# A layer with linear attention and a gated MLP on one core: query features token-major and normalised, turned by DMA; KV sums and numerators in blocks of three heads; a new order of the units

## The chip, the cores and the metric

The kernel runs on one core of a Trainium2 chip. A core has a matrix engine (TensorE, PE in the profile, with its weight loads as PEld), a vector engine (DVE), a scalar engine (ACT), GpSimd (POOL), a synchronisation engine that mainly issues transfers (SP), and 16 DMA engines. The engines run their own instruction streams in order and wait for each other on semaphores. Matrices are multiplied from SBUF into PSUM (eight banks of 512 fp32 columns). The metric is device microseconds of one execution, as a median of several runs. A profiled execution tells where the time goes.

## What is computed

One sequence of 2048 tokens, width 640, 32 heads of 20, all in bf16 at the borders. The layer norm has no learned scale.

```python
def _A_ref(x, wqkv, w_phi, wo):
    H = 32; Dh = D // H
    q, k, v = ...                      # x @ wqkv, split into heads
    pq = jnp.einsum("bhsd,hdf->bhsf", q, w_phi)
    pk = jnp.einsum("bhsd,hdf->bhsf", k, w_phi)
    phi_q = jnp.concatenate([_softmax(pq, axis=-1), _softmax(-pq, axis=-1)], axis=-1)
    phi_k = jnp.concatenate([_softmax(pk, axis=-1), _softmax(-pk, axis=-1)], axis=-1)
    kv = jnp.einsum("bhsf,bhsd->bhfd", phi_k, v)
    z  = jnp.einsum("bhsf->bhf", phi_k)
    num = jnp.einsum("bhqf,bhfd->bhqd", phi_q, kv)
    den = jnp.einsum("bhqf,bhf->bhq", phi_q, z)[..., None] + 1e-6
    return (num / den) ... @ wo
...
h = x + _A_ref(_layernorm(x), ...)
g, u = _layernorm(h) @ w_gate, _layernorm(h) @ w_up     # 640 -> 1536
return h + (g * u) @ w_down                             # 1536 -> 640
```

So each head has 40 features per token: a softmax over 20 numbers and a softmax over their negatives. The KV sum runs over all tokens, so no numerator can be made before the last key tile has been added.

## The kernel before

**Tiles.** 16 token tiles of 128 tokens. Weights of q and k are first multiplied with `w_phi` ("folds", `F1_*` for k and `F0_*` for q, L389), so that features come from one projection. For the folds, K weights are transposed on TensorE (`WT`, L370) and Q weights by DMA (`wqt`, L302).

**Key and value side, per token tile t.** `L1*` and `xn` normalise the tile; `xt` transposes it, for the first four tiles on TensorE (L451), for the others by a DMA on SP's queue (L460). `V` and `K` (L473) are token-major projections: ten matmuls of 320 columns into two PSUM banks, split into five parts for tiles 0 and 1. ACT makes exp(+) and exp(-) of the K projection (`Kx`, L494) into `ek`; DVE sums each group of 20 (`Ks`, L497); ACT makes the reciprocals by Ln and Exp (`Kr`, `Ke`); POOL multiplies (`Kn`, L504). `KV` (L513) adds the tile to the KV sum: 128 feature columns of one sign are the weights, the values of the heads that these 128 columns touch are the moving side (21 columns a head, the 21st being ones, for z). 128 columns touch 7 or 8 heads of 20, and both signs lie apart, so a tile takes 12 matmuls with 1512 columns in all, into three banks. Products of a head's features with another head's values are masked off with `GL` at the end (`KVe`, L520).

**Query side.** `Q` (L534) is feature-major: 20 units, one for each 512 tokens and 128 features, of five matmuls of 512 columns. ACT writes exp(+) and exp(-) straight into `eqT` (`Qx`, L543), which stays unnormalised and needs no transpose. `N` (L567) makes the numerators of a tile, for each sign apart: six matmuls a sign, 22 columns a head (values, z, and a column of ones that gives the softmax sum). DVE then joins the signs, six instructions a tile: `sr` (L580), `rho` (L582), `A` (L585), `B` (L588), `dd` (L592), `rd` (L596); `o` (L599) multiplies with the reciprocal, on POOL or DVE.

**After that, per tile.** `oT` (L604) transposes `o` by DMA, `O` (L610) multiplies with `wo`, `h` (L614) adds x, `L2*` and `hc` make the second layer norm, `hT` (L637) transposes it by DMA into `xnT`, in place of the tile's first normalised copy.

**MLP.** Five blocks of tokens `FB` (256, 512, 512, 512, 256). `U` units (L652) are five matmuls each, gate and up; `g` (ACT, L657) copies the gate, `u` (DVE, L660) multiplies; `D` (L671) is the down projection of a tile, 24 matmuls of 320 columns; `y` (L683) adds h, `w` (L685) stores. `wd` loads `w_down` into the space of the q, k and v weights, and so waits for the last projection.

**Order.** `build_graph` makes named operations, with their engine. The list `TUNED` gives each a number; `schedule` walks through the graph in the order of these numbers and assigns buffers, `emit` turns dependencies into semaphore waits. What is built is one fixed list of instructions for each engine: each engine, SP's queue too, runs its list in order, so one that waits holds all behind it.

Of the kernel before, what the change touches and what calls it, by code (L numbers as in the profile page):

```python
# [12 lines left out]
P = 128  # L13
# [16 lines left out]
for _s in range(2):  # L30
    for _c in range(NC):
        OFF[_s, _c] = _o
        _o += NH[_c]
NSLOT = _o
BSLOT = NSLOT // 3

QB = [(512 * b, 512) for b in range(4)]
# [18 lines left out]
L1a12:33.687 L1s13:28.597 L1a13:31.337 L1s14:33.797 L1a14:35.117 L1s15:26.247 L1a15:28.487 L1l0:7.437 L1e0:7.867 L1l1:4.317 L1e1:4.747 L1l2:11.156
L1e2:11.586 L1n2:11.896 L1n3:12.096 L1l4:15.157 L1e4:16.001 L1n4:16.711 L1n5:16.511 L1n6:16.311 L1n7:16.911 L1l8:26.088 L1e8:26.667 L1n8:28.855
L1n9:31.414 L1n10:31.814 L1n11:31.614 L1l12:35.45 L1e12:35.88 L1n12:39.691 L1n13:36.932 L1n14:36.732 L1n15:39.491 xn0:8.226 xt0:9.088 xte0:9.853
xn1:5.057 xt1:5.737 xte1:6.905:1 xn2:12.348 xt2:13.039 xte2:13.911 xn3:12.574:1 xt3:13.59 xte3:15.748:1 xn4:17.487 xt4:20.107 xn5:17.348:1 xt5:18.887
xn6:16.987 xt6:17.667 xn7:17.987 xt7:21.327 xn8:29.417 xt8:30.097 xn9:31.764:1 xt9:32.687 xn10:33.25:1 xt10:35.127 xn11:34.617 xt11:36.347 xn12:40.341  # L60
xt12:41.227 xn13:37.588:1 xt13:40.007 xn14:37.082 xt14:38.787 xn15:39.841 xt15:44.887 V0_0:10.806 V0_1:11.078 V0_2:11.681 V0_3:11.953 V0_4:12.496
Ve0:13.287 K0_0:14.141 K0_1:14.412 K0_2:14.684 K0_3:14.956 K0_4:15.227 Kx0_0:16.101 Kx0_1:18.684 Ks0:19.907 Kr0:21.568 Ke0:22.431 Kn0:24.137 KV0:29.083
V1_0:9.44 V1_1:9.712 V1_2:12.224 V1_3:12.768 V1_4:13.869 Ve1:14.534 K1_0:7.713 K1_1:8.817 K1_2:10.263 K1_3:10.534 K1_4:13.318 Kx1_0:15.377 Kx1_1:16.724
Ks1:18.487 Kr1:20.554 Ke1:21.418 Kn1:21.778 KV1:29.759 V2:19.574 Ve2:24.691 K2:15.499 Kx2_0:18.061 Kx2_1:19.308 Ks2:21.327 Kr2:23.204 Ke2:25.314
Kn2:26.496 KV2:33.151 V3:16.857 Ve3:19.931 K3:18.216 Kx3_0:20.794 Kx3_1:21.808 Ks3:24.827 Kr3:26.427 Ke3:27.39 Kn3:29.055 KV3:33.827 V4:30.435
Ve4:32.477 K4:26.366 Kx4_0:27.994 Kx4_1:28.907 Ks4:29.917 Kr4:31.517 Ke4:33.1 Kn4:34.373 KV4:37.22 V5:23.649 Ve5:25.464 K5:27.724 Kx5_0:30.029
Kx5_1:30.862 Ks5:32.267 Kr5:34.587 Ke5:35.67 Kn5:37.132 KV5:40.613 V6:22.291 Ve6:24.068 K6:20.933 Kx6_0:22.581 Kx6_1:23.444 Ks6:27.067 Kr6:28.667
Ke6:29.53 Kn6:32.014 KV6:45.364 V7:25.008 Ve7:26.767 K7:31.793 Kx7_0:33.963 Kx7_1:34.827 Ks7:35.66 Kr7:38.302 Ke7:38.752 Kn7:39.891 KV7:47.398
V8:35.862 Ve8:37.582:1 K8:34.503 Kx8_0:36.132 Kx8_1:36.965 Ks8:38.333 Kr8:40.148 Ke8:41.011 Kn8:42.25 KV8:48.389 V9:39.254 Ve9:40.883:1 K9:37.896
Kx9_0:39.524 Kx9_1:40.388 Ks9:41.634 Kr9:43.54 Ke9:43.99 Kn9:44.609 KV9:49.065 V10:41.289 Ve10:42.917 K10:42.647 Kx10_0:44.275 Kx10_1:45.109  # L70
Ks10:45.942 Kr10:47.542 Ke10:48.405 Kn10:48.765 KV10:52.789 V11:54.824 Ve11:56.452:1 K11:46.04 Kx11_0:47.782 Kx11_1:48.615 Ks11:49.449 Kr11:51.085
Ke11:51.535 Kn11:53.483 KV11:60.257 V12:53.465 Ve12:55.207 K12:50.072 Kx12_0:51.7 Kx12_1:52.534 Ks12:53.367 Kr12:54.967 Ke12:55.83 Kn12:56.19
KV12:60.933 V13:58.899 Ve13:60.527:1 K13:51.43 Kx13_0:53.157 Kx13_1:53.99 Ks13:54.824 Kr13:56.424 Ke13:56.874 Kn13:58.549 KV13:62.239 V14:56.182
Ve14:57.81 K14:44.005 Kx14_0:45.732 Kx14_1:46.565 Ks14:47.399 Kr14:49.862 Ke14:50.312 Kn14:51.124 KV14:62.915 V15:63.906 Ve15:65.534 K15:57.54
Kx15_0:59.169 Kx15_1:60.002 Ks15:61.279 Kr15:62.879 Ke15:63.329 Kn15:63.689 KV15:68.502 KVe0:70.058 KVe1:70.668 KVe2:69.448 F0_0:48.074 Fe0_0:49.239
F0_1:61.609 Fe0_1:62.194 F0_2:63.591 Fe0_2:64.176 F0_3:49.741 Fe0_3:50.462 F0_4:61.924 Fe0_4:62.699:1 Q0_0:70.257 Qx0_0_0:71.606 Qx0_0_1:72.123
Q0_1:67.423 Qx0_1_0:69.288 Qx0_1_1:68.772 Q0_2:69.178 Qx0_2_0:70.527 Qx0_2_1:71.044 Q0_3:66.343 Qx0_3_0:67.693 Qx0_3_1:68.209 Q0_4:65.264 Qx0_4_0:67.13
Qx0_4_1:66.613 Q1_0:74.529 Qx1_0_0:75.879 Qx1_0_1:76.395 Q1_1:76.689 Qx1_1_0:78.039 Qx1_1_1:78.555 Q1_2:73.45 Qx1_2_0:75.316 Qx1_2_1:74.799 Q1_3:91.923
Qx1_3_0:93.974 Qx1_3_1:93.457 Q1_4:78.459 Qx1_4_0:80.324 Qx1_4_1:79.808 Q2_0:88.34 Qx2_0_0:90.357 Qx2_0_1:90.874 Q2_1:71.336 Qx2_1_0:72.685
Qx2_1_1:73.202 Q2_2:90.844 Qx2_2_0:92.94 Qx2_2_1:92.424 Q2_3:89.764 Qx2_3_0:91.39 Qx2_3_1:91.907 Q2_4:82.041 Qx2_4_0:83.39 Qx2_4_1:83.907 Q3_0:79.538  # L80
Qx3_0_0:80.887 Qx3_0_1:81.404 Q3_1:80.617 Qx3_1_0:82.483 Qx3_1_1:81.966 Q3_2:87.261 Qx3_2_0:89.84 Qx3_2_1:88.61 Q3_3:75.61 Qx3_3_0:76.959
Qx3_3_1:77.476 Q3_4:83.12 Qx3_4_0:84.469 Qx3_4_1:84.986 wd0:94.712 wd1:94.232 wd2:93.272 wd3:93.752 N0_1:73.105 N0_0:72.415 sr0:73.72 rho0:74.21
A0:74.58 B0:75.61 dd0:76.64 rd0:77.03 o0:77.51:1 oT0:78.422 O0:84.199 h0:86.035 L2s0:87.087 L2a0:88.659 L2v0:88.949 L2r0:89.659 hc0:89.127 hT0:90.05
N1_1:77.769 N1_0:72.76 sr1:78.384 rho1:78.874 A1:79.244 B1:80.274 dd1:81.304 rd1:81.694 o1:82.174:1 oT1:83.085 O1:85.903 h1:87.907 L2s1:88.839
L2a1:89.839 L2v1:90.129 L2r1:90.844 hc1:90.344:1 hT1:91.27 N2_1:89.419 N2_0:85.558 sr2:90.034 rho2:90.974 A2:91.344 B2:92.374 dd2:93.404 rd2:93.794
o2:94.274 oT2:95.695 O2:103.382 h2:105.142 L2s2:106.555 L2a2:107.727 L2v2:108.017 L2r2:111.472 hc2:108.017 hT2:108.94 N3_1:81.696 N3_0:78.114
sr3:82.905 rho3:83.395 A3:83.765 B3:84.795 dd3:85.825 rd3:86.787 o3:87.267 oT3:88.688 O3:93.002 h3:94.63 L2s3:95.692 L2a3:96.702 L2v3:96.992
L2r3:97.732 hc3:97.261 hT3:98.184 N4_1:94.36 N4_0:94.705 sr4:95.382 rho4:96.512 A4:96.882 B4:98.214 dd4:99.415 rd4:99.805 o4:100.457:1 oT4:101.369
O4:112.592 h4:114.437 L2s4:115.369 L2a4:116.369 L2v4:116.659 L2r4:117.159 hc4:116.659:1 hT4:117.622 N5_1:100.308 N5_0:98.325 sr5:101.189 rho5:101.679
A5:102.049 B5:103.25 dd5:104.452 rd5:104.842 o5:105.322 oT5:106.743 O5:110.889 h5:112.555 L2s5:113.617 L2a5:115.189 L2v5:115.479 L2r5:116.189  # L90
hc5:115.479 hT5:116.402 N6_1:105.286 N6_0:106.177 sr6:106.245 rho6:107.837 A6:108.207 B6:109.409 dd6:110.61 rd6:111.172 o6:111.652 oT6:113.073
O6:120.47 h6:122.099 L2s6:123.04 L2a6:124.71 L2v6:125 L2r6:125.74 hc6:125.87:1 hT6:126.55 N7_1:145.093 N7_0:143.669 sr7:145.981 rho7:146.471 A7:146.841
# [132 lines left out]
def build_graph():  # L225
# [329 lines left out]
    for t in range(NT):  # L555
# [18 lines left out]
        def nv(b, lo, hi):  # L574
            return pp(b, 0, 352).rearrange("p b (h e) -> p b h e", e=22)[:, :, :, lo:hi]
# [457 lines left out]
```

## Time and profile before

| | us |
|---|---|
| median of 3 runs (281.85 to 282.33) | 282.11 |
| span of the profiled execution | 281.1 |
| TensorE busy in it | 274.9 |
| DVE busy | 176.8 |
| ACT busy | 109.6 |
| POOL busy | 61.3 |
| DMA queue 1, share of 16 engines | 28.9% |

| group | instructions | busy, us | mean of one, ns |
|---|---|---|---|
| `KV` L513, TensorE | 192 | 12.7 | 218 |
| `N` L567, TensorE | 192 | 15.7 | 221 |
| `Q` L534, TensorE | 96 (of 100) | 21.9 | 379 |
| `Ks` L497, DVE | 16 | 23.3 | 1475 |
| `Kn` L504, POOL | 16 | 37.4 | 2358 |
| `Qx` L543, ACT | 40 | 21.4 | 598 |
| `A`, `B` L585 and L588, DVE | 16 each | 13.7 each | 854 |
| `xt`, `hT` L460 and L637, SP | 28 | - | - |

The mean of one matmul is longer than the distance between two starts, since matmuls overlap; the distance is read from the chain of waits or from the starts. A transpose on SP is an issue of some 1.2 us, and the data move after it; the DMA issues of the page give the time to landing.

### The profile page before, as it was taken

The page shows a single profiled execution, that of the slowest core. Times are in us where ns is not written, and L with a number is a line of the kernel's source. Part 1 is how long each engine was busy: PE and PEld are TensorE (multiplying, and loading weights), DVE is VectorE, ACT ScalarE, POOL GpSimd, SP SyncE. Part 2 cuts the span into 40 slices and gives each one's busy share as a digit, 9 for nine tenths or more (in the row PEclk, how much of TensorE's full clock was granted, in tenths as well). Part 3 has the DMA queues.
Part 4 walks back from the last instruction along what each step waited for, and adds up shares of the span by engine and source line. Part 5 has one row for each costly group of instructions (what it writes and reads, how often), then busy time and mean ns, then how long its engine had stood idle before and what let it go on. Part 6 is the DMA issues. An engine that isn't in the chain of part 4 may idle for free.

```text
span 281.1 us, 5047 instructions
## 1 busy us (share of the span) xinstructions
PE 274.9 (98%) x2058; PEld 182.7 (65%) x2075; DVE 176.8 (63%) x357; ACT 109.6 (39%) x217; POOL 61.3 (22%) x78
## 2 busy tenths in 40 slices
PE   7899999999999999999999999999999999999996
PEld 3677777876556688765555675545675554587874
DVE  5899986542588798855888974338725452341532
ACT  3799876846785742112311301303200203330200
POOL 6017998873002102202012000010110200000000
PEclk9999999999999999999999999999999999999999
DMA  7923276990011692232111342010141230000001
GB/s 211 369 56 74 53 131 113 313 372 8 0 26 31 153 261 48 41 79 49 25 23 26 70 106 60 0 23 2 25 97 47 40 32 23 0 2 23 26 34 60
DMA packets 43479, 21.98 MB, mean 78 GB/s; under 512 B 34624, under 2 KB 42176, under 8 KB 43456
## 3 DMA queue, kind: packets, MB, share of 16 engines
q1 hardware_dynamic: 42080, 20.02, 28.9%
q10 hardware_dynamic: 1376, 1.64, 1.9%
q8 instruction: 16, 0.26, 0.4%
q14 instruction: 7, 0.06, 0.1%
HBM read 11.00 MB, written 2.62 MB: 48 GB/s over the span
## 4 chain that ended last, share of the span: by engine, by line
PE 95%; DMA 2%; DVE 1%; issue 0%; ACTq 0%; ACT 0%; POOL 0%; DVEq 0%
PE ps L652 36%; PE ps L671 19%; PE ps L473 16%; PE ps L610 8%; PE ps L534 8%; PE ps L567 4%; PE ps L513 4%; DMA scratch<-in_A_wqkv_dram 2%; PE ps L389 1%; PE ps L370 0%; PE ps L451 0%; DVE x_all L614 0%; DVE ev L660 0%; DVE st L620 0%; ACTq L274 0%
## 5 line engine op out<-in xcount | busy, mean ns | idle before, releaser
L652 PE MATMUL ps<-xnT,Wgu 128*128 128x512 bf16 (+1 forms) x587 | 106.4, 335 | 0.7
L652 PEld LDWEIGHTS ps<-xnT,Wgu 128*128 128x128 bf16 x600 | 58.1, 98 | 41.7 <-DVE ev L660 0.6
L657 ACT ACTIVATE scratch<-ps 128x512 bf16<-128x512 f32 (+1 forms) x60 | 30.7, 512 | 117.4 <-PE ps L652 98.5
L660 DVE TENSOR_TENSOR ev<-ps,scratch 128x512 bf16<-128x512 f32 (+1 forms) x60 | 33.6, 579 | 34.5 <-ACT scratch L657 18.7
L671 PE MATMUL ps<-Wp,ev 128*128 128x320 bf16 (+2 forms) x396 | 53.5, 295 | 0.0
L671 PEld LDWEIGHTS ps<-Wp,ev 128*128 128x128 bf16 x396 | 38.0, 98 | 14.1
L473 PE MATMUL ps<-Wp,xnT 128*128 128x320 bf16 x320 | 45.9, 299 | 0.0
L504 POOL TENSOR_TENSOR ev<-ev,SR 128x1280 bf16<-128x1280 bf16 x16 | 37.4, 2358 | 9.5 <-ACT SR L502 9.5
L473 PEld LDWEIGHTS ps<-Wp,xnT 128*128 128x128 bf16 x320 | 30.7, 98 | 11.2
L599 POOL TENSOR_TENSOR scratch<-scratch,sm 128x640 bf16<-128x640 f32 x10 | 12.7, 1273 | 94.9 <-DVE sm L596 91.7
L683 DVE SCALAR_TENSOR_TENSOR Wp<-ps,rs,x_all 128x640 bf16<-128x640 f32 (+3 forms) x18 | 14.5, 808 | 30.0 <-PE ps L671 30.0
L497 DVE TENSOR_REDUCE SR<-ev 128x64 f32<-128x1280 bf16 x16 | 23.3, 1475 | 6.2 <-ACT ev L494 6.1
L610 PE MATMUL ps<-Wo,scratch 128*128 128x320 bf16 x160 | 24.0, 299 | 0.0
L543 ACT ACTIVATE eqT<-ps 128x512 bf16<-128x512 f32 x40 | 21.4, 598 | 6.2 <-PE ps L534 6.2
L494 ACT ACTIVATE ev<-ps 128x640 bf16<-128x640 f32 x32 | 21.6, 713 | 4.2 <-PE ps L473 3.6
L534 PE MATMUL ps<-xnT,Wp 128*128 128x512 bf16 x96 | 21.9, 379 | 0.2
L610 PEld LDWEIGHTS ps<-Wo,scratch 128*128 128x128 bf16 x160 | 15.6, 98 | 7.0 <-issue 0.2
L614 DVE TENSOR_TENSOR x_all<-ps,x_all 128x640 bf16<-128x640 f32 x16 | 12.9, 813 | 7.8 <-PE ps L610 7.8
L534 PEld LDWEIGHTS ps<-xnT,Wp 128*128 128x128 bf16 x100 | 9.6, 98 | 10.3
L567 PE MATMUL ps<-KVm,eqT 128*128 128x154 bf16 (+1 forms) x192 | 15.7, 221 | 0.0
L567 PEld LDWEIGHTS ps<-KVm,eqT 128*128 128x128 bf16 x192 | 13.0, 98 | 4.0
L624 POOL TENSOR_SCALAR ln<-mv 128x1 f32<-128x1 f32 x16 | 3.3, 210 | 49.4 <-DVE mv L623 47.3
(59 smaller groups left out, 204.4 us busy)
## 6 DMA issues: line engine op xcount, KB each, us to landing
out_dram<-Wp SPq DMA_DIRECT2D x15, 160.0 KB, 1.8
x_all<-in_A_x_dram SPq DMA_DIRECT2D x6, 320.0 KB, 10.0
Wgu<-in_B_w_up_dram SPq DMA_DIRECT2D x5, 384.0 KB, 7.7
Wgu<-in_B_w_gate_dram SPq DMA_DIRECT2D x5, 384.0 KB, 6.1
Wp<-in_B_w_down_dram SPq DMA_DIRECT2D x4, 480.0 KB, 5.2
scratch<-in_A_wqkv_dram ACTq DMA_DIRECT2D x2, 320.0 KB, 5.5
Wo<-in_A_wo_dram SPq DMA_DIRECT2D x1, 480.0 KB, 9.0
xnT<-xn SPq DMA_TRANSPOSE x28, 2.7
```

The source lines that it names most:

```text
L473: ins = e.matmul(pb(b, hb)[:, 0:320], lhsT=T["xnT"][:, NC - 1 - c, P * t:P * (t + 1)], rhs=T["Wp"][:, kind, c, 320 * hb:320 * (hb + 1)], s ...
L494: G.op("act", "Kx%d_%d" % (t, s), lambda e, s=s, b=b, ek=ek: e.activation(out=T["ek"][:, ek.slots[0], s, :].rearrange("p (b n) -> p b n", ...
L497: G.op("dve", "Ks%d" % t, lambda e, ek=ek, sr=sr: e.tensor_reduce(out=T["SR"][:, sr.slots[0], 0, :], in_=T["ek"][:, ek.slots[0], :, :].rea ...
L504: G.op("pool", "Kn%d" % t, lambda e, ek=ek, sr=sr: e.tensor_tensor(out=T["ek"][:, ek.slots[0], :, :].rearrange("p s (h f) -> p (s h) f", f ...
L534: ins = e.matmul(pb(b)[:, 0:n], lhsT=T["Wp"][:, 0, i, P * c:P * (c + 1)], rhs=T["xnT"][:, NC - 1 - i, o0:o0 + n], start=(i == 0), stop=(i ...
L543: G.op("act", "Qx%d_%d_%d" % (q, c, s), lambda e, s=s, c=c, o0=o0, n=n, b=b: e.activation(out=T["eqT"][:, s, c, o0:o0 + n], in_=pb(b)[:, 0 ...
L567: ins = e.matmul(pb(b, y)[:, 22 * h0:22 * (h0 + j1 - j0)], lhsT=T["eqT"][:, s, c, P * t:P * (t + 1)], rhs=T["KVm"][:, OFF[s, c] + j0:OFF[s ...
L610: ins = e.matmul(pb(b, hb)[:, 0:320], lhsT=T["oT"][:, oT.slots[0], c, :], rhs=T["Wo"][:, c, 320 * hb:320 * (hb + 1)], start=(c == 0), stop ...
L652: ins = e.matmul(pb(b)[:, 0:n], lhsT=T["Wgu"][:, gu, c, P * ft:P * (ft + 1)], rhs=T["xnT"][:, NC - 1 - c, o0:o0 + n], start=(c == 0), stop ...
L657: G.op("act", "g%d_%d" % (bi, ft), lambda e, pg=pg, gt=gt, n=n: e.activation(out=T["gt"][:, gt.slots[0], 0:n], in_=pb(pg)[:, 0:n], func=AF ...
L660: o_ = G.op("dve", "u%d_%d" % (bi, ft), lambda e, pu=pu, gt=gt, hh=hh, ft=ft, n=n: e.tensor_tensor(out=T["hh"][:, hh.slots[0], ft, 0:n], i ...
L671: ins = e.matmul(pb(b, hb)[:, 0:w], lhsT=T["hh"][:, hh.slots[0], ft, P * tt:P * (tt + 1)], rhs=T["Wd"][:, ft, c0 + w * hb:c0 + w * (hb + 1 ...
```

## The change

**Query features.** `Q` becomes a token-major projection like K and V, 16 units of ten matmuls of 320 columns. `feat` (new, used for K and Q) makes exp, sums and reciprocals, now with a head's two signs side by side, 40 columns a head. `Qn` multiplies into a buffer `ph` of 11 blocks of 128 columns (three heads are 120 columns, the rest is zeros), on POOL for twelve tiles and on DVE for tiles 0, 1, 2 and 11. `qT` turns all 11 blocks with one DMA transpose on SP's queue.

**KV and numerators.** Weights are 128 columns that hold three heads with both signs; the moving side is these three heads, 63 columns (42 for the last two heads). Eleven matmuls a tile for `KV`, twelve for `N` (block 5 lies across two banks and is split). Two KV banks in place of three. `N` comes once, normalised, so `sr`, `rho`, `A`, `B` go, and `dd`, `rd`, `o` read PSUM; `o` is always on DVE.

**Placement and order.** `eqT`, `A`, `B` go, `ph` (4 buffers), `phT` (5) and a mask come; `ek` has 7 buffers in place of 6, and `SR` 4 in place of 3. The weights of q come last in `Wp`, so that `wd0` to `wd2` wait for the K and V projections alone, `wd3` for Q too. A new list `PLAN` gives every operation a number, its engine and its buffers; `arrange` sorts by the number in place of `schedule`.

```diff
-QB = [(512 * b, 512) for b in range(4)]
+NB = 11
+BW = [120 * g for g in range(10)] + [1152]
+BH = [3] * 10 + [2]
+POS = {1: 0, 2: 1, 0: 2}
...
+    def feat(nm, t, b, kk):
...
+            G.op("act", "%sx%d_%d" % (nm, t, s), lambda e, s=s, b=b, ek=ek: e.activation(
+                out=T["ek"][:, ek.slots[0], :].rearrange("p (b h s f) -> p b h s f", b=2, s=2, f=DH)[:, :, :, s, :],
+                in_=pp(b, 0, 320).rearrange("p b (h f) -> p b h f", f=DH), func=AF.Exp,
+                scale=1.0 - 2.0 * s), act_c(640), LA, [b], [ek], kk)
+        G.op("dve", "%ss%d" % (nm, t), lambda e, ek=ek, sr=sr: e.tensor_reduce(
...
         def kv(e, t=t, ek=ek, va=va):
-            for k in range(3):
-                for n, (s, c, j0, j1, sl) in enumerate(ent[k]):
...
+            for g in range(NB):
+                n = 21 * BH[g]
+                ins = e.matmul(pb(KVB[g // 8])[:, 63 * (g % 8):63 * (g % 8) + n], lhsT=T["ek"][:, ek.slots[0], BW[g]:BW[g] + P],
+                               rhs=T["va"][:, va.slots[0], 63 * g:63 * g + n],
+                               start=(t == 0 and g % 8 == 0), stop=(t == NT - 1), skip_group_check=True)
...
+    for t in range(NT):
+        kk = 165 + 8 * t
+        b = proj(0, t, "Q%d" % t, kk)
+        ek, sr = feat("Q", t, b, kk)
+        ph = Buf("ph%d" % t, "ph")
+        def qn(e, eng, ek=ek, sr=sr, ph=ph):
...
+            e.tensor_tensor(
+                out=o_[:, 0:10 * P].rearrange("p (g n) -> p g n", n=P)[:, :, 0:120].rearrange("p g (h f) -> p g h f", f=DH),
+                in0=i_[:, 0:1200].rearrange("p (g h f) -> p g h f", h=6, f=DH),
+                in1=r_[:, 0:60].rearrange("p (g h) -> p g h", h=6).unsqueeze(3).to_broadcast([P, 10, 6, DH]), op=ALU.mult)
+            return e.tensor_tensor(
...
+        G.op("sp", "qT%d" % t, lambda e, ph=ph, phT=phT: e.dma_start_transpose(
+            out=T["phT"][:, phT.slots[0], :, :], in_=T["ph"][:, ph.slots[0], :]), 2.6, 0.0, [ph], [phT], kk, dma=-2.2)
     for k in range(4):
         dma("sp", "wd%d" % k, lambda k=k: T["Wd"][:, 3 * k:3 * k + 3, :],
...
-            after=lastproj)
+            after=kvprojs if k < 3 else projs)
...
+            for g in range(NB):
+                for h0, h1 in [(3 * g, 3 * g + BH[g])] if g != 5 else [(15, 16), (16, 18)]:
+                    y = h0 // 16
+                    ins = e.matmul(pb(b, y)[:, 21 * (h0 - 16 * y):21 * (h1 - 16 * y)], lhsT=T["phT"][:, phT.slots[0], g, :],
+                                   rhs=T["KVm"][:, h0:h1, :].rearrange("p h e -> p (h e)"),
...
-        G.op("dve", "sr%d" % t, ...
-        G.op("dve", "rho%d" % t, ...
-        G.op("dve", "A%d" % t, ...
-        G.op("dve", "B%d" % t, ...
...
+        G.op("dve", "o%d" % t, lambda e, sm=sm, b=b, o=o: e.tensor_tensor(
+            out=T["o"][:, o.slots[0], :].rearrange("p (b h d) -> p b h d", b=2, d=DH), in0=nv(b, 0, 20),
...
-        order, _ = schedule(G)
+        order = arrange(G)
```

The parts of the new lists that the prediction speaks of, in the order in which the engines run them:

```
SP, start:       x0 x1 wk4 x2 w5 wk2 wk0 wv0 x4 wv2 x6 x14 wv4 x8 x12 x10   (before: two queues, SP and ACT)
POOL, start:     all three Phi products on POOL (before: two on DVE), with the mask among the selects
SP, then:        ... xt15 xt12 wqt4 wu3 wo2 wu0 wg2 wu4 wu1 wg0 wg1 wu2 wo0 wg3 xt13 wg4 xt14 qT2 qT5 qT0 qT1
SP, from V13:    wd1 wd0 wd2 qT4 qT8 oT0 oT1 qT3 qT7 oT4 oT5 oT2 hT0 hT1 qT15 qT6 oT3 qT12 wd3 oT8 hT4 oT7 qT14
                 hT2 hT5 hT3 qT13 qT10 qT9 w1 hT8 qT11 oT15 hT7 oT6 oT10 w0 oT14 oT13 hT6 ...
PE, V9 to K14:   V9 F0_0 KV4 V10 F0_2 F0_4 KV5 KV6 F0_1 F0_3 K11 K15 Q2 Q5 KV7 KV8 Q0, Q1 (in parts) KV9 K12 KV10 K14
PE, from V13:    V13 Q3 KV13 KV14 KV15 Q15 N0 N1 Q9 Q11 N2 N4 Q10 Q13 O0 N5 Q12 N8 O1 N3 Q14 O4 O5 O2 N7
                 24 units U0, with O3 among them, then O8 N6 O7 N15 D1 U1 U1 D0 N14 U1 U1 N10 U1 U1 N11 ...
```

The first unit of U0 needs `hT0` and `hT1`; the first of U1 needs `hT2` to `hT5`. After the last N and O, TensorE has only U and D units left.

## The prediction, made before the changed kernel was run

> **What bounds the kernel now.** I read the page's busy times first, then the slices, then the chain of waits.
>
> ```profile
> PE 274.9 (98%) x2058; PEld 182.7 (65%) x2075; DVE 176.8 (63%) x357; ACT 109.6 (39%) x217; POOL 61.3 (22%) x78
> ...
> PE   7899999999999999999999999999999999999996
> ...
> PEclk9999999999999999999999999999999999999999
> ...
> PE 95%; DMA 2%; DVE 1%; issue 0%; ACTq 0%; ACT 0%; POOL 0%; DVEq 0%
> ```
>
> TensorE is busy from the second slice to the last, at full clock, and it is 95% of the chain. From 15.3 us to the last matmul at 278.3 no start lies later than its predecessor's columns explain; seventeen gaps of 0.22 us are one missing record each. So the end is the start-up, plus the sum of the matmul work, plus whatever idle time a change puts in. The price of the work stands in the chain of waits in order of time:
>
> ```profile
> 30.73 1.36 PE ps L513 x24
> 32.09 2.72 PE ps L473 x20
> ...
> 142.81 0.71 PE ps L567 x12
> 143.52 2.16 PE ps L652 x10
> ...
> 150.71 1.36 PE ps L610 x10
> ```
>
> Columns are: start, us, what, count. Two KV tiles of 12 matmuls (L513) take 1.36, so 0.68 a tile; a projection of ten 320-column matmuls (L473, L610) takes 1.36, 136 ns each; the numerators of a tile (L567) take 0.71; a 512-column matmul (L652, likewise the Q unit L534) takes 216 ns.
>
> **The change, part by part. TensorE.** KV per tile goes from 12 matmuls with 1512 columns to 11 with 672 (ten of 63, one of 42); the numerators from 12 with 1584 columns to 12 with 672. No row has 63 columns. In single starts of the trace a 42-column matmul of L513 holds PE for 29 ns (median of 32), the 80-column ones of L389 for 35 ns, each with a weight load of its own. So 63 lies between 29 and 35; 63 columns at the 42-to-80 slope would be 32, but 80 columns cost 33.3 at 2.4 columns a ns plus 2, and 63 by that is 28. I take 30. KV: 0.68 - 11 x 0.030 = 0.35 less a tile, 5.6 us over 16. Numerators: 0.71 - 0.36 = 0.35, 5.6 us. Q was 100 matmuls of 216 ns = 21.6, and is 160 of 136 = 21.8: 0.2 more. **Net -11.0** (-11.4 at 29 ns, -9.3 at 35).
>
> One rule speaks against this. The Trainium skill, "TensorE: Matmul & The Clock Gate", Back-to-back issue gap, gives some 81 ns per matmul for a stream of weight-load and 128-column matmul pairs; the 128-column transposes L370 and L451 here start 56 ns apart, so the row decides. By the page an estimate for KV would be 11 x 81 = 0.89 us a tile, above the 0.68 of now, and the change would lose on TensorE.
>
> **Vector, scalar and GpSimd work.** DVE loses the two 672-wide passes (L585, L588, 13.7 us each), `sr` and `rho` (5.7 + 2.9) and six `o`; it gains 16 reductions `Qs` (L497's row, 1475 ns: 23.6), 16 `o` from PSUM (L614's row, 813 ns: 13.0) and four `Qn` (about 1.5). ACT trades 40 Exp of 598 ns for 32 of 713 and gets 32 small ones of 0.26; the evictions of V (L238, 711 ns), which write runs of 20 elements already, show that the interleaved output costs no more. POOL trades ten `o` (1273) for twelve `Qn` (by L504's 2358 ns for 1280 elements: about 2.5). `Kn` and `Qn` together are 16 x 2.36 + 12 x 2.5 = 68 us of POOL, from the first Exp pair at some 20 us to `Qn13` at some 110. None of this is on the path while TensorE has other units ready, and I cost it at nothing; what it costs if the cover fails is rival 2, DVE being the fullest of the three between 70 and 125 us.
>
> **SP's queue.** This is where the cover is thin. Each `qT` turns 11 blocks of 128x128, against five in every transpose there is now.
>
> ```profile
> xnT<-xn SPq DMA_TRANSPOSE x28, 2.7
> ...
> 36.29 2.60 SPq L460 DMA_TRANSPOSE xnT<-xn  x2
> 38.93 1.27 SPq L302 DMA_TRANSPOSE scratch<-in_A_wqkv_dram  x1
> 40.24 4.54 SPq L460 DMA_TRANSPOSE xnT<-xn  x3
> ```
>
> The first line is from the DMA issues, the others from the timeline of SP. A five-block transpose holds SP for 1.20 us alone and 1.27 in a dense row, where starts lie 1.31 apart; its packets run from 1.17 to 2.13 us after the issue (0.96 us of transfer) and it lands at 2.7. Eleven blocks aren't shown. If the issue costs per instruction, one holds SP for 1.3; if per block, 11/5 x 1.20 = 2.64 and 0.04 between; if per block as in the slowest instruction there is (the one at 41.57 us took 1.90), 4.2. I take 2.68, since the transfer starts only when the issue is over, as if the issue wrote the descriptors one after another. It lands 2.1 (transfer) + 0.45 later.
>
> In the new order SP works through, after the last K/V projection V13 has freed `Wd`'s space, up to `qT11`: 12 `qT`, 15 five-block transposes, four `wd` and one output. That is 12 x 2.68 + 15 x 1.31 + 2.3 + 2.5 for the last landing = 56.6 us. TensorE's units from V13 to N11, the numerators that wait for `qT11`, are 16 Q and O (21.8), 3 KV (1.0), 12 N (4.3), 24 U0 (0.545 each: 13.1), 2 D (L671, 3.26: 6.5) and 6 U1 (1.08: 6.5): 53.2. **SP is 3.4 us longer than the work that hides it: +3.4 of idle TensorE.** Behind a `qT` that waits stand the `oT` and `hT` that feed O and U, so these come late by the same. At 1.3 per `qT` it is hidden (0); at 2.85 (dense rows) it is 5.4; at 4.2 it is 21.7. The same sum up to `hT1`, before the first U0, gives 21.5 of work against 4 x 2.68 + 7 x 1.31 + 1.5 + 1.4 = 22.8: there the first 1.3 of it show.
>
> "Advanced Engine Details and Errata" of the Trainium skill, X-Bar Transpose (TRN2), says that transposing DMAs are as fast as plain ones, 350 to 400 GB/s. Here 160 KB took 0.96 us, 171 GB/s. By the page an estimate for the 352 KB of a `qT` is 0.95 us in place of 2.1, and the idle time would be 2.3.
>
> **Loads behind which work now waits.** `xt13` and `xt14` are issued behind the Wo, gate and up loads. Those 4.7 MB now go from the first issue at 48.78 to landed data at 63.2, 14.4 us; two transposes add 2 x 0.96 + 0.45: 16.8. Where the loads begin in the new order TensorE is at V9; from there to K14, which needs `xt14`, are nine projections (12.2), five Q folds (1.6) and seven KV (2.3): 16.1. So +0.7 (0 to 1.6).
>
> **Start-up.** All input loads go through SP alone, K weights ahead of V's. In the present trace TensorE waits for K weights until 8.41 (chain: L370) and the last V weights land at 12.8, behind x tiles that aren't needed yet; then it is dense from 15.3. The bytes ahead of the last V weights fall to 3.3 MB, at some 350 GB/s from 2 us on: 11.5 to 12. All three `Phi` products (658 ns on POOL) now stand on POOL behind its memsets and selects, some 5.9 us by their rows in all after 0.8, so at 6.7; the K folds need them at about 7.3, K weights landed, turned and copied. I take -0.5 (-1.5 to +1.0: one queue in place of two, or POOL, may come late).
>
> **Sum.** 281.1 (span) - 11.0 + 3.4 + 0.7 - 0.5 = 273.7. The median of the runs is 1.0 above the span, so **274.7 us**.
>
> **The rivals.** (1) *The transposes are hidden after all* (issue under 2.4 us): the idle 3.4 goes. Time: 271.3. For it: SP is free for long stretches in the present trace; against it: a dense queue with 12 of the new kind. 0.25.
> (2) *DVE becomes the bound in that stretch.* From `Qs6` to `Qn11`, which feeds `qT11`, the new order has 10 reductions (1.40 start to start), 9 `o` and 8 `h` (0.74), 8 pairs of statistics (0.75), 12 `u` (0.335) and small ones: 45.9 us back to back, and 5.2 for `qT11` makes 51.1, under 53.2. At the use DVE reaches in its busiest stretch now (33.29 of 40.00 us between 17 and 57) it takes 55.3 + 5.2 = 60.5: idle 7.3 instead of 3.4, time 278.6. 0.09.
> (3) *Narrow matmuls don't go under the 56 ns of 128 columns.* KV 0.62, N 0.67: TensorE saves 1.4 in all, and its longer units hide SP's 3.4 and the loads' 0.7. Time: 281.1 - 1.4 - 0.5 + 1.0 = 280.2. Against it: the rows of 42 and 80. 0.05.
> (4) *The other side: the 11-block transposes hold SP at the rate of its slowest one*, 4.2 us. Place: the queue from V13 to `qT11`; idle 21.7 instead of 3.4; time 293. It decides from 3.4 + 7.4 = 10.8 us of idle, that is 0.6 us more per `qT` than I take: 3.3. For it: instructions of 1.3 to 1.9 in dense rows; against: one in 49. 0.11.
>
> **How the numbers follow.** The forecast holds 0.48, with 272.5 to 277.5 as its own range; 0.02 is left for no change. A difference under 0.2% (0.6 us) can't be told from none here. Faster: 0.48 + 0.25 + 0.09 + 0.05 = 0.87; slower 0.11. The range takes in (1) less some start-up gain and goes to (3): 270.4 to 280.3.
>
> **What would show it.** L513's and L567's successors at some 0.33 and 0.36 us a tile in the chain; the `qT` lines on SP at 2.6 to 2.7 us; SP without a pause between V13 and `qT11`; holes in TensorE of together 3 to 5 us before the first U0, before U1 and at N11, released by a transpose, and none after about 130 us. No holes, or `qT` at 2.4 or less, means (1). Holes released by DVE mean (2). A gap of 50 ns between 63-column matmuls means (3). `qT` above 3.3 us makes the forecast wrong in sign.

## The result, and the profile after

The changed kernel takes **284.1 us** (median of 7 runs, 283.21 to 285.96); the kernel before took 282.11 in the same session (7 runs, 281.85 to 283.05). The ratio is 1.007, 95% interval 1.0042 to 1.0098: slower by 0.7%, where 2.6% faster was forecast. Here and below a ratio leaves out runs that lie more than 1.5% above the same kernel's fastest, while medians and ranges are of all runs. The profiled execution has a span of 283.5 us. The parts of its page that were read before:

```profile
PE 268.4 (95%) x2119; PEld 179.0 (63%) x2119; DVE 181.1 (64%) x324; ACT 113.3 (40%) x241; POOL 82.6 (29%) x99
...
PE   6999997998939989999999999999999999999996
...
PEclk9999997999988999999999999999999999999999
...
PE 72%; DMA 11%; DVE 8%; issue 3%; ACT 2%; POOL 2%; SPq 1%; DVEq 0%
```

The TensorE line, without a break before, now has breaks in slices 7, 10, 12 and 15, all between 42 and 107 us; the clock line dips in slices 7, 12 and 13; and the chain that ended last is only 72% TensorE. From slice 16 on the kernel is as dense as it was. So the saving and the loss lie in different places, and the saving can be read by itself, in the chain of waits of the changed kernel (start, us, what, count):

```profile
56.71 0.68 PE ps L525 x22
...
106.16 0.35 PE ps L578 x12
```

Two KV tiles of 11 matmuls (L525) take 0.68, 0.34 a tile where it was 0.68 a tile; the numerators (L578) take 0.35 in place of 0.71. The matmul work has become 11 us shorter, as the sum had it. What it met instead stands in TensorE's timeline between 30 and 150 us, in the brackets: idle time before the line, and what ended it.

```profile
33.51 4.25 PE L481 MATMUL ps<-Wp,xnT 128*128 128x320 bf16 x30 [0.48 <-DMA xnT<-xn]
45.53 0.74 PE L408 MATMUL ps<-Phi,scratch 128*128 128x140 bf16 x6 [1.99 <-DMA scratch<-in_A_wqkv_dram]
69.12 4.25 PE L481 MATMUL ps<-Wp,xnT 128*128 128x320 bf16 x30 [1.20 <-ACT ev L250]
83.73 1.86 PE L525 MATMUL ps<-ev,ek 128*128 128x63 bf16 x33 [4.59 <-DVE ev L250]
91.44 0.52 PE L578 MATMUL ps<-KVm,scratch 128*128 128x63 bf16 x12 [0.17 <-DMA scratch<-ph]
103.27 2.89 PE L604 MATMUL ps<-Wo,scratch 128*128 128x320 bf16 x20 [0.72 <-DMA scratch<-o]
```

The largest wait, 4.59 us, is ended by the copy of a V projection on VectorE (L250), and the next, 1.99, by a transpose of Wq out of DRAM. Three small ones are ended by transposes out of SBUF, of which the forecast's sum had counted the last two, a `qT` and an `oT`. At the two large holes TensorE went to half clock: the granted clock is 0.50 from 45.59 to 49.00 us and from 83.13 to 86.55, 3.41 us each time. In these stretches 320-column matmuls started 266 ns apart in place of 136, and 63-column ones 53 in place of 32; the same matmuls took 1.6 and 1.2 us longer than at full clock.

Measured from the distances of matmul starts, each less its own columns at 2.4 a ns and 2.5 ns (single missing records left out), TensorE's idle time per stretch is, in us (what half clock adds counts as idle here):

| kernel | 5 to 16 | 30 to 60 | 60 to 90 | 90 to 150 | last matmul ends |
|---|---|---|---|---|---|
| before | 1.7 | 0.2 | 0.2 | 0.3 | 278.5 |
| changed | 2.4 | 4.7 | 7.6 | 2.3 | 281.2 |

Why VectorE copied V13 so late is seen on VectorE and GpSimd together. L497 is the group sum of the features, L549 and L553 are the two multiplies of a `Qn` (1200 and 80 columns), L517 is `Kn`. From the timeline of the changed kernel:

```profile
61.60 2.40 DVE L553 TENSOR_TENSOR ph<-ek,SR 128x80 bf16<-128x80 bf16 x1
...
69.49 2.01 DVE L549 TENSOR_TENSOR ph<-ek,SR 128x1200 bf16<-128x1200 bf16 x1
...
71.95 4.67 POOL L517 TENSOR_TENSOR ek<-ek,SR 128x1280 bf16<-128x1280 bf16 x2 [1.70 <-ACT SR L502]
...
74.37 3.52 DVE L549 TENSOR_TENSOR ph<-ek,SR 128x1200 bf16<-128x1200 bf16 x1
...
76.58 3.39 POOL L549 TENSOR_TENSOR ph<-ek,SR 128x1200 bf16<-128x1200 bf16 x1
77.81 2.25 DVE L553 TENSOR_TENSOR ph<-ek,SR 128x80 bf16<-128x80 bf16 x1
...
82.77 0.81 DVE L250 CAST ev<-ps 128x640 bf16<-128x640 f32 x1
```

An 80-column multiply of 0.23 us takes 2.40 and 2.25; the 1200-column one, 1.41 alone (at 130 us, when GpSimd rests), takes 2.01 and 3.52. GpSimd's own multiply beside them takes 3.39 in place of 2.22. The times interlock: GpSimd's two `Kn` end at 76.62; VectorE's multiply, issued at 74.37, ends 1.27 us later at 77.89; GpSimd's `Qn`, issued at 76.58, ends 2.08 us after that; and VectorE's 80 columns end 0.09 us after it. The excess on VectorE is 2.2 us for `Qn2`, 0.6 for `Qn0` and 4.1 for `Qn1`: 6.9 us, just ahead of the copy that TensorE waits for.

The theory: **a VectorE multiply with two inputs in SBUF and a GpSimd multiply exclude each other for whole instructions.** The Trainium skill states this, on the page "SBUF — State Buffer", Who interferes with whom: a VectorE instruction with two SBUF inputs contends with a GpSimd instruction that reads SBUF, the later one is held up until the other has ended, and a `tensor_reduce` never contends. The trace agrees: no L497 was longer than 1.49. The rivals: VectorE merely has too much work there; or SP's queue of transposes sets the pace, as the forecast had it.

### The profile page after: what moved, and what is told of

Same layout as the page of the kernel before. It is cut to its first block, busy times and chain, and to the rows that moved or that the text cites. A ratio compares the mean times of both kernels' runs of the same rounds, so it can differ in the third digit from the quotient of the medians.

```text
span 283.5 us, 5219 instructions
## 1 busy us (share of the span) xinstructions
PE 268.4 (95%) x2119; PEld 179.0 (63%) x2119; DVE 181.1 (64%) x324; ACT 113.3 (40%) x241; POOL 82.6 (29%) x99
## 4 chain that ended last, share of the span: by engine, by line
PE 72%; DMA 11%; DVE 8%; issue 3%; ACT 2%; POOL 2%; SPq 1%; DVEq 0%
PE ps L646 35%; PE ps L665 18%; PE ps L481 8%; PE ps L604 6%; DMA scratch<-ph 4%; DVE SR L497 3%; DMA scratch<-o 3%; DMA scratch<-in_A_wqkv_dram 3%; POOL ek L517 2%; DVE ph L549 2%; DMA xnT<-xn 1%; ACT ek L493 1%; PE ps L408 1%; PE ps L578 1%; SPq L284 1%
## 5 line engine op out<-in xcount | busy, mean ns | idle before, releaser
L651 ACT ACTIVATE gt<-ps 128x512 bf16<-128x512 f32 (+1 forms) x60 | 30.6, 512 | 104.2 <-PE ps L646 65.3
L481 PE MATMUL ps<-Wp,xnT 128*128 128x320 bf16 x480 | 70.4, 303 | 1.7 <-ACT ev L250 1.2
L654 DVE TENSOR_TENSOR ev<-ps,gt 128x512 bf16<-128x512 f32 (+1 forms) x60 | 33.3, 578 | 42.8 <-PE ps L646 28.6
L481 PEld LDWEIGHTS ps<-Wp,xnT 128*128 128x128 bf16 x480 | 46.2, 99 | 19.7 <-ACT ev L250 1.5
L497 DVE TENSOR_REDUCE SR<-ek 128x64 f32<-128x1280 bf16 x32 | 46.7, 1474 | 2.2 <-ACT ek L493 2.2
L493 ACT ACTIVATE ek<-ps 128x640 bf16<-128x640 f32 x64 | 43.3, 701 | 11.5 <-PE ps L481 7.1
L517 POOL TENSOR_TENSOR ek<-ek,SR 128x1280 bf16<-128x1280 bf16 x16 | 38.7, 2434 | 15.4 <-ACT SR L502 15.4
L549 POOL TENSOR_TENSOR ph<-ek,SR 128x1200 bf16<-128x1200 bf16 x12 | 27.8, 2319 | 14.1 <-ACT SR L502 10.6
L594 DVE TENSOR_TENSOR o<-ps,sm 128x640 bf16<-128x640 f32 x16 | 12.8, 808 | 3.2 <-DMA scratch<-o 3.1
L525 PE MATMUL ps<-ev,ek 128*128 128x63 bf16 (+1 forms) x176 | 8.1, 204 | 4.6 <-DVE ev L250 4.6
L525 PEld LDWEIGHTS ps<-ev,ek 128*128 128x128 bf16 x176 | 7.8, 106 | 5.5 <-issue 4.9
L250 ACT ACTIVATE ev<-ps 128x640 bf16<-128x640 f32 x13 | 9.2, 707 | 2.2 <-PE ps L481 2.2
```

Of the source, the lines that this page charges most:

```text
L481: ins = e.matmul(pb(b, hb)[:, 0:320], lhsT=T["xnT"][:, NC - 1 - c, P * t:P * (t + 1)], rhs=T["Wp"][:, POS[kind], c, 320 * hb:320 * (hb + 1 ...
L493: G.op("act", "%sx%d_%d" % (nm, t, s), lambda e, s=s, b=b, ek=ek: e.activation(out=T["ek"][:, ek.slots[0], :].rearrange("p (b h s f) -> p ...
L497: G.op("dve", "%ss%d" % (nm, t), lambda e, ek=ek, sr=sr: e.tensor_reduce(out=T["SR"][:, sr.slots[0], 0, :], in_=T["ek"][:, ek.slots[0], :] ...
L517: G.op("pool", "Kn%d" % t, lambda e, ek=ek, sr=sr: e.tensor_tensor(out=T["ek"][:, ek.slots[0], :].rearrange("p (h f) -> p h f", f=DH), in0 ...
L525: ins = e.matmul(pb(KVB[g // 8])[:, 63 * (g % 8):63 * (g % 8) + n], lhsT=T["ek"][:, ek.slots[0], BW[g]:BW[g] + P], rhs=T["va"][:, va.slots ...
L549: e.tensor_tensor(out=o_[:, 0:10 * P].rearrange("p (g n) -> p g n", n=P)[:, :, 0:120].rearrange("p g (h f) -> p g h f", f=DH), in0=i_[:, 0 ...
```

## The experiments

**One input in place of two.** The three `Qn` that run on VectorE beside GpSimd get an operation of the same length and place, with one input:

```diff
+            if t < 3:
+                e.tensor_reduce(out=o_[:, 0:10 * P].rearrange("p (g n) -> p g n", n=P)[:, :, 0:120],
+                                in_=i_[:, 0:1200].rearrange("p (g n o) -> p g n o", n=120, o=1), axis=AX.X, op=ALU.add)
+                return e.tensor_reduce(out=o_[:, 11 * P - 80:11 * P],
+                                       in_=i_[:, 1200:1280].rearrange("p (n o) -> p n o", o=1), axis=AX.X, op=ALU.add)
             e.tensor_tensor(
```

> The Qn operations of tiles 0, 1 and 2, which VectorE does in this kernel while GpSimd multiplies, are replaced by a tensor_reduce over an axis of one element: same engine, same place, same output buffer, and about the same length alone (1.47 us for 128x1280 in the trace against 1.41), but one input instead of two. It leaves out the normalisation of these three tiles' query features. Theory (a VectorE operation with two SBUF inputs and a GpSimd multiply exclude each other): the three lose their excess of about 7 us, the TensorE holes at 67.6 (1.37 us) and 78.8 (4.76 us and 0.5 us of half clock after it) close, and the time falls by 5 to 7 us to 277 to 279. Rival (VectorE simply has too much work in 45 to 80 us): the work is as long as before, both holes stay, 283.5 to 284.7. Rival (the query transposes on SP's queue set the pace): no change either, 283.5 to 284.7.

Measured: 280.49 us (276.95 to 281.44, 4 runs), ratio to the kernel before 0.988 (0.9809 to 0.995). The waits for V14's buffers (1.37 us by starts) and V13's copy (4.76) are gone from the trace, and VectorE's busy time falls from 181.1 to 174.4 us, by about the excess. The profiled run, 276.95, is at the lower edge of the theory's range, the median 1.5 us above the upper one. In the profiled run the hole at 43.25 was 1.72 us and the clock stayed full throughout; the other three runs had mean clocks of 0.988 and 0.994 and took 280.1 to 281.4. There are no traces of those three, so where they lost clock, and whether that is all of their 3 to 4.5 us, is not shown.

**Wq transposes early, alone and with the first edit.** In the order table:

```diff
-wqt0:29.816 wqt1:32.256 wqt2:34.696 wqt3:27.376 wqt4:38.43
+wqt0:12.0 wqt1:12.5 wqt2:13.0 wqt3:13.5 wqt4:14.0
```

> The five transposes of Wq out of DRAM are put at the head of SP's queue of transposes (order numbers 12 to 14 instead of 27 to 38); nothing else moves. Theory (the hole at 43.24 of 2.15 us is the fold's wait for the fifth of them, and the half clock at 46.7 to 48.5, about 1 us, follows from it): both go, and what they made late comes 3 us earlier. If nothing later eats it the time is 281; if the VectorE and GpSimd exclusion of 60 to 80 us binds anyway, part of it is given back: 281 to 283.5. Rival (the hole belongs to the fold's evacuations or to the queue itself): 284 or, by 12 us more of issue ahead of the first xn transposes, later than 284.

> Both edits: one-input operations in place of the Qn of tiles 0 to 2 (their normalisation is left out) and the Wq transposes at the head of the queue. Theory: the two holes are independent causes, about 6 and 3 us: 274 to 276, which is what the prediction's sum would have given without them. Rival (one cause behind the other, so that the second hides the first): no better than the better of the two alone, 277 to 279.

Measured: alone 281.8 (280.75 to 284.27, 10 runs; ratio 0.9985, 0.9956 to 1.0014), both 277.49 (276.33 to 277.73, 4 runs; ratio 0.9802, 0.9768 to 0.9836). Against the changed kernel's 1.007 that is 0.8% for the transposes, 1.9% for the one-input operations (uncertain by 0.7 either way) and 2.7% for both: within the intervals they add up. The 277.49 itself lies above the theory's range and inside the rival's; what speaks against the rival is that each edit alone measured more, and the traces: with one-input operations alone the hole at 43.25 remains (1.72 us), with early transposes alone the one before the `KV` of tile 13 (4.75), and with both neither does. In the kernel with both, the same stretch of VectorE and GpSimd, where L550 and L552 are the replacements, reads:

```profile
68.76 4.67 POOL L517 TENSOR_TENSOR ek<-ek,SR 128x1280 bf16<-128x1280 bf16 x2 [1.86 <-ACT SR L502]
69.79 1.39 DVE L550 TENSOR_REDUCE ph<-ek 128x1200 bf16<-128x1200 bf16 x1
71.10 0.23 DVE L552 TENSOR_REDUCE ph<-ek 128x80 bf16<-128x80 bf16 x1
```

Both run in the middle of two `Kn` and nobody is held up: 1.39 and 0.23, and two `Kn` in 4.67. VectorE's amount of work is unchanged, so that rival falls.

**The operations by themselves.** In place of the computation, the list of phases is (VectorE's operations, GpSimd's operations), each phase begun when the last is over:

```python
PH = [([qn] * 4, []), ([], [kn] * 4), ([qn] * 6, [kn] * 4), ([rd] * 4, []), ([rd] * 6, [kn] * 4),
      ([lambda e: qn(e, ps[:, 0:64])] * 4, []), ([lambda e: qn(e, ps[:, 0:64])] * 6, [kn] * 4),
      ([xn] * 6, []), ([xn] * 12, [kn] * 4), ([ob] * 6, []), ([ob] * 10, [kn] * 4)]
```

> The disputed operations by themselves; the whole computation is left out and the output is zeros. VectorE runs, first alone and then beside four GpSimd multiplies of 128x1280 (Kn's form): the Qn multiply from SBUF, the group sum Qs, the Qn multiply with the reciprocals in PSUM, the one-input xn operation in bf16, and the o multiply from PSUM. SP issues three transposes of 11 blocks and three of 5 blocks, each waited for. Theory of exclusion: the Qn form is 1.41 alone, and beside GpSimd six of them and four multiplies take the sum of both, 6x1.41 + 4x2.36 = 17.9 us, with single instructions of up to 3.8 us; the sum Qs, the form with a PSUM input and o stay at their lengths. Rival (ordinary sharing of bandwidth or none): the six take 8.5 to 11 us and no form differs from another. Transposes: 11 blocks 1.37 us to issue and 3.5 to land, 5 blocks 1.2 to 1.3 and 2.6.

From the groups of instructions by form, first the stretch of 23 to 40 us (`Qn`'s form beside `Kn`'s; the fifth L56 is the end of the phase before), then lines of the whole run (busy us, mean ns):

```profile
L39 DVE TENSOR_TENSOR ph_dve<-ek_dve,sr_dve 128x1200 bf16<-128x1200 bf16 x6 | 16.6, 2837 | 9.7 <-POOL kn_pool L56 9.7
L56 POOL TENSOR_TENSOR kn_pool<-ek_pool,sr_pool 128x1280 bf16<-128x1280 bf16 x5 | 16.4, 3299 | 0.1
```

```profile
L48 DVE TENSOR_SCALAR xn_dve<-z,sc 128x640 bf16<-128x640 bf16 x18 | 14.7, 892 | 1.6 <-POOL kn_pool L56 1.6
L45 DVE TENSOR_REDUCE red<-ek_dve 128x64 f32<-128x1280 bf16 x10 | 14.1, 1479 | 0.1
L39 DVE TENSOR_TENSOR ph_dve<-ek_dve,ps 128x1200 bf16<-128x1200 bf16 x10 | 13.3, 1400 | 1.2 <-POOL kn_pool L56 1.1
L51 DVE TENSOR_TENSOR xn_dve<-ps,sr_dve 128x640 bf16<-128x640 f32 x16 | 11.9, 815 | 0.1
```

Six `Qn` beside four `Kn` take 16.6 us, where the theory gave 17.9 with both in a row and the rival 8.5 to 11. In single records they alternate strictly: while both engines have work, every `Qn` but the first shows 3.55 us and every `Kn` after its first 3.51, the sum of the two less the overlap of their ends. The sum (L45, 1479 alone and beside `Kn`), the same `Qn` with its reciprocals in PSUM (1400) and `o` from PSUM (815) stay at their lengths. One line wasn't in the expectation: the one-input `xn` in bf16 (L48) took 0.44 alone and 2.47 beside `Kn`, so two inputs aren't the only way into the exclusion. The kernel's own `xn`, which writes its blocks in reverse order, takes 0.55 to 0.61 with or without GpSimd, so it isn't concerned. The three 11-block transposes took 1.35 to 1.40 to issue and 3.6 to land, the 5-block ones 1.20 and 2.6.

**Only the copy that was waited for.** One token of the table puts V13's copy on ScalarE:

```diff
-Ve13:70.291:1:2
+Ve13:70.291::2
```

> The changed kernel with one token of the order table changed: the copy of tile 13's values (Ve13), for which the hole at 78.84 waits, is taken by ScalarE instead of VectorE. Everything is computed and the three Qn stay on VectorE beside GpSimd. Theory (the copy was only the first thing found behind a VectorE that is several us late): the next wait takes its place, for Kn13 on GpSimd, for the KV evacuations on VectorE behind Qn1 or for tile 1's query transpose, and at most 1 to 2 us are gained: 282.5 to 284.2. Rival (the placing of that one copy is the fault, not the exclusion): the hole of 4.8 us goes and the time is 279 to 280.

Measured: 283.4 (283.09 to 284.47, 8 runs), ratio 1.004 (1.0024 to 1.0057). TensorE has a wait of nearly the same length in the old place, and ScalarE's lines in the timeline show why:

```profile
78.11 0.70 ACT L493 ACTIVATE ek<-ps 128x640 bf16<-128x640 f32 x1 [3.49 <-DVE ph L553]
...
80.19 0.70 ACT L250 ACTIVATE ev<-ps 128x640 bf16<-128x640 f32 x1
...
81.03 1.72 PE L525 MATMUL ps<-ev,ek 128*128 128x63 bf16 x33 [3.94 <-ACT SR L502]
```

It is still the wait for V13's copy. ScalarE makes it from 80.19 to 80.89, and TensorE starts 0.14 us after its end, much as it did behind VectorE's copy in the changed kernel. L502, which the profile names, ended only as TensorE started, and the last `Kn` had ended at 74.57. ScalarE works through its list in order, and ahead of the copy stands an exp that waited 3.49 us for the second part of `Qn1` on VectorE (L553, until 78.02). So the copy went to another engine and stayed behind the same stall, though not by one of the waits that the expectation named. The gain is 0.7 us, no more than the width of the intervals.

**GpSimd's multiply in quarters.** The exclusion holds for whole instructions, so shorter ones should hold less. `Kn` of tiles 11 to 15 is cut, with the Wq transposes early; everything is computed:

```diff
+            k = 4 if t in (11, 12, 13, 14, 15) else 1
+            for a in range(0, 64, 64 // k):
+                z = a + 64 // k
+                ins = e.tensor_tensor(
+                    out=T["ek"][:, ek.slots[0], DH * a:DH * z].rearrange("p (h f) -> p h f", f=DH),
...
+                    in1=T["SR"][:, sr.slots[0], 1, a:z].unsqueeze(2).to_broadcast([P, z - a, DH]), op=ALU.mult)
```

> GpSimd's multiply Kn of tiles 11 to 15 is cut into four of 128x320 instead of one of 128x1280, with the Wq transposes at the head of the queue as before; everything is computed. Theory of exclusion: VectorE's Qn now waits for at most one quarter, about 0.7 us instead of 2.36, and the three Qn lose about 3 us instead of 7, though GpSimd pays about 0.5 us more for each Kn: 1 to 3 us faster than with the early Wq transposes alone (281.8), so 279 to 281. Rival (the loss is VectorE's amount of work): GpSimd's extra 2.5 us only delays KV, 282 to 284.

Measured: 278.67 (276.83 to 282.87, 10 runs), ratio 0.986 (0.9838 to 0.9882), a little better than expected. Timeline, L521 the quarters, L555 and L559 the two parts of a `Qn` on VectorE:

```profile
65.93 3.26 POOL L521 TENSOR_TENSOR ek<-ek,SR 128x320 bf16<-128x320 bf16 x3
66.63 1.97 DVE L555 TENSOR_TENSOR ph<-ek,SR 128x1200 bf16<-128x1200 bf16 x1
68.53 0.76 DVE L559 TENSOR_TENSOR ph<-ek,SR 128x80 bf16<-128x80 bf16 x1
...
72.09 1.42 DVE L555 TENSOR_TENSOR ph<-ek,SR 128x1200 bf16<-128x1200 bf16 x1
73.43 0.76 DVE L559 TENSOR_TENSOR ph<-ek,SR 128x80 bf16<-128x80 bf16 x1
```

`Qn` now loses at most one quarter (0.72 us) at each of its two parts: 2.7 and 2.2 us in place of 5.8 for the worst. Three quarters in 3.26 show the other side: one of them waited for VectorE's 1.4.

**Short query transposes.** On the kernel with both edits each `qT` turns 2 of 11 blocks (the others are left out):

```diff
-            out=T["phT"][:, phT.slots[0], :, :], in_=T["ph"][:, ph.slots[0], :]), 2.6,
+            out=T["phT"][:, phT.slots[0], 0:2, :], in_=T["ph"][:, ph.slots[0], 0:2 * P]), 2.6,
```

> As the kernel with both edits (one-input operations in place of the Qn of tiles 0 to 2, Wq transposes early), and every query transpose turns 2 of its 11 blocks only; the other nine are left out. Theory (with the VectorE stall gone, what is left of the holes, 1.7 us of N's wait for a query transpose at 84 and 0.5 to 0.6 at 95.6 and 60, is SP's queue, the prediction's 3.4 us): 2 to 3 us faster than with both edits (277.5), 274.5 to 275.5. Rival (the transposes are hidden and N waits for something else): 277 to 278.

Measured: 275.26 (274.52 to 276.76, 4 runs), ratio 0.9755 (0.9721 to 0.9789); with both edits and whole transposes it was 0.9802. By the medians 2.2 us, but the intervals overlap, and in the traces only N's wait for a query transpose becomes shorter, from 1.71 to 0.72 us, the others by 0.2 or not at all; 1.5 us of the difference of the two traces lies in the start-up. So about 1 us is shown to be the size of these transposes, and the rest is open.

**New order tables.** Four kernels compute everything and have a table in which the order of each engine was worked out anew with the exclusion in it, from the durations in the traces, the last two with `Kn` in quarters as well. A few tokens of the third (name, order number, second engine or not, buffer), which among others puts V13's copy and `xn14` on ScalarE, `Qn11` on GpSimd and `Qn12` on VectorE:

```diff
-wqt4:38.43 xt14:46.738 xn14:46.058::1 Ve13:70.291:1:2 Qn11:115.846:1:1 Qn12:94.258::0
+wqt4:26.8668 xt14:46.0294 xn14:45.1061:1:3 Ve13:72.8386::3 Qn11:113.1679::2 Qn12:127.7741:1:0
```

> The kernel's instructions as they are, everything computed; only the order table is new (order numbers, some buffer numbers, and which engine takes some evacuations and Qn). The order was worked out from the durations and landing times of these traces, with the rule that a Qn on VectorE and a GpSimd multiply exclude each other. By the same working the changed kernel's last matmul ends at 281.5 (trace: 281.2) and this one's at 272.2. Theory: 9 us less than the changed kernel, 274 to 277. Rival (other waits than those in the working decide, so that any new order only moves them): 280 to 286.

> A second order of the same kind, found from another start: last matmul at 273.1 by the same working. Theory: 275 to 278. Rival: 280 to 286.

> Everything is computed. The kernel with Kn of tiles 11 to 15 in quarters, and a new order table worked out from the traces' durations with the exclusion of Qn on VectorE and GpSimd's multiplies, and with 0.6 us of slack for every transpose; it also moves some evacuations between ScalarE and VectorE, and Qn12 and Qn13 to VectorE at times when GpSimd has less to do. By the same working the kernel in quarters has its last matmul at 275.9 (trace: 274.5 or so by its span of 277.4) and this one at about 271. Theory: 3 to 5 us faster than quarters alone (278.7), 273.5 to 276. Rival (the order table isn't what is left, as with the first new order, which fell 4 us behind its working): 278 to 281.

> A second table of the same kind from another start, also at about 271 by the same working; it keeps more evacuations where they were and puts the weight loads between the transposes of the normalised tokens. Theory: 273.5 to 276. Rival: 278 to 281.

Measured, against the kernel before of the same session:

| kernel | us, median | ratio, 95% interval |
|---|---|---|
| first table | 279.38 (4 runs) | 0.9897 (0.9879 to 0.9915) |
| second table | 281.6 (10 runs) | 0.9968 (0.9939 to 0.9997) |
| third, `Kn` in quarters | 277.4 (5 runs) | 0.9814 (0.9791 to 0.9836) |
| fourth, `Kn` in quarters | 277.42 (6 runs) | 0.9821 (0.9779 to 0.9862) |

All lie above the theory's ranges, the first two by 2.4 and 3.6 us, the last two, worked out with slack for every transpose, by 1.4. In the trace of the first, TensorE was idle 4.1 us between 5 and 16 us (2.4 in the changed kernel), in part because of half clock from 9.12 to 12.54, and it waited 1.02 us for VectorE at 90.4 and 0.82 for a transpose of `o` at 96.6. The third and the fourth are the best versions found that compute everything; the third is 1.9% faster than the kernel before and 2.5% faster than the change as it was made. Against quarters in the old order it gains 0.5%, no more than the width of the intervals.

## Why the prediction was wrong

**The failed step** is the paragraph "Vector, scalar and GpSimd work", with its "None of this is on the path while TensorE has other units ready, and I cost it at nothing". It priced the four `Qn` on VectorE at "about 1.5" each and never asked what GpSimd does in the same microseconds. The trace of before held such a pair only once, in the start-up. There a `Phi` product on VectorE, with two inputs in SBUF, was issued at 4.26 us, while GpSimd's own product ran from 4.14 to 4.80:

```profile
L358 DVE TENSOR_TENSOR Phi<-w,GL 128x280 bf16<-128x280 bf16 x1 | 0.8, 837 | 0.0
```

By the lengths of `Qn`'s two parts alone (0.23 us for 80 columns, 1.41 for 1200) 280 columns would be about 0.44 us, an estimate. The six `o` on VectorE, which also read two SBUF operands, took 811 to 826 ns at times when GpSimd rested, and give no price. But the text itself counted 68 us of `Kn` and `Qn` on GpSimd between 20 and 110 us, so three `Qn` of tiles 0 to 2 were likely to fall on them. Cost: 6.9 us of VectorE, of which TensorE saw 6.1 in the two holes (1.37 and 4.76 by starts), and 1.2 more in half clock; 1.9% by the first experiment.

**A step that was left out.** The folds of Wq wait for five transposes out of DRAM that the new table puts between the `xt` on SP's queue. The forecast priced the loads behind them, not the folds ahead. Cost: a hole of 2.15 us and 1.6 us of half clock; 0.8% (2.3 us) by the second experiment, in whose trace the half clock at the other hole lasted 6.83 us in place of 3.41.

**TensorE, -11.0.** Right: 0.34 and 0.35 a tile against 0.35 and 0.36 in the sum. 63-column matmuls start 32 ns apart (median), not 30, and the rival of narrow matmuls at 56 ns is out.

**SP's queue, +3.4.** Its working was wrong; that its size is not far off is luck. A `qT` by itself is issued in 1.35 to 1.40 us, not 2.68 (median in the changed kernel 1.40): the issue costs per instruction, and 11 blocks cost 0.2 us more than 5. By the forecast's own words ("`qT` at 2.4 or less") that means rival 1, transposes hidden. They aren't quite: a `qT` lands 3.8 us after its issue (median), and N, O and the first U units waited 0.3 to 0.9 us at a time, 2.0 us more than before between 90 and 150 us. With the other causes gone, 1.71 and 0.49 us of waits for a `qT` and an `oT` remain. About 1 us of that goes with the size of the `qT`, as the experiment with short ones shows; why the rest isn't hidden stays open. Rival 4, 4.2 us per issue, is out as well, though the side it stood for came true, by another cause.

**Rival 2, VectorE as the bound,** named the right engine in the wrong place: it looked between `Qs6` and `Qn11`, by adding up lengths. VectorE was late at `Qn2` to `Qn1` (60 to 80 us), by lengths that weren't their own.

**Loads, +0.7.** K14's wait for `xt14` is 0.62 us with both edits and 1.25 in the kernel with quarters; in the changed kernel itself the earlier holes hid it.

**Start-up, -0.5.** Not seen: TensorE was busy 12.79 us of the first 16, against 13.33 before, and its idle time from 5 to 16 us was 2.4 us against 1.7 (1.9 to 4.7 in the traces of the other kernels, the highest ones with half clock in that stretch).

Without the two costs that were missed, the forecast would have held, though only just: both edits together gave 277.49, at the edge of its own range of 272.5 to 277.5 and 2.8 us above its value. In that kernel's trace the start-up alone has 4 us of idle time between 5 and 16 us, part of it half clock, where 1.7 were there before and a gain was forecast.

## What to carry to other kernels

When a change puts a VectorE operation with two SBUF inputs into a stretch in which GpSimd multiplies, price it by the sum of both lengths, and each instruction of it separately: an 80-column remainder of 0.23 us lost 2.2 us, as much as its large sibling. Three ways out were measured: one input in PSUM (no loss at all), an operation with one input that does not contend (a sum does not, the plain bf16 `xn` does), or shorter GpSimd instructions (at most one quarter lost each time). And where the profile names an engine that came late, look at what made its earlier instructions longer than elsewhere before the named one is moved, and check the named one by its end: one that ends only when the waiting engine starts did not release it.

## What was not expected of the hardware

- Both sides of the exclusion show as busy time, not as idle: `Kn` 3.51 us in place of 2.35, `Qn` 3.55 in place of 1.41. Busy shares therefore look healthier than they are; only the length of one instruction against the same form elsewhere gives it away.
- Half clock came in stretches of 3.41 us, and once of 6.83. Holes in TensorE of 2.15, 4.11 and 4.75 us brought it; holes of 1.72, 1.84 and 1.9 us in other runs did not, but neither did holes of 2.46 and 2.21 us in the trace of the second new order table. So the length of a hole alone doesn't decide. "TensorE: Matmul & The Clock Gate" of the Trainium skill, What's actually happening, speaks of an idle window of some 3.4 us. The stretches here are as long as that, but a hole of 2.15 us sufficed; what decides is not shown.
- A transpose of 11 blocks costs SP's queue hardly more than one of 5: 1.35 to 1.40 against 1.20 us.
